# Attention's values of each head's first unit by 64 queries, in halves of the columns of TensorE's array

## The chip, the cores and the metric

One core of a Trainium2 chip runs the whole program. The metric is the device time of one execution in microseconds (us), median over several runs; the profile is of one more execution, recorded by the hardware profiler. TensorE (PE) multiplies a moving operand by weights that a separate instruction, LDWEIGHTS, has put into its 128 x 128 array; the profile shows the weight loads as an engine of their own (PEld). VectorE is DVE, ScalarE is ACT, GpSimd is POOL, and SP issues nearly all transfers.

## The reference, cut to what matters

The kernel computes a gated mix of two branches over 2048 tokens of width 576: an attention with a compressive memory (32 heads of 18 columns, four segments of 512 tokens), and a feed-forward block of 4608 hidden columns.

```python
logits = jnp.einsum("bhqd,bhkd->bhqk", qs, ks) * scale + mask   # causal, inside a segment
p = _softmax(logits, axis=-1)
a_dot = jnp.einsum("bhqk,bhkd->bhqd", p, vs)                    # the values
...
o = g * a_mem + (1.0 - g) * a_dot
...
b = (_gelu(x @ w_gate) * (x @ w_up)) @ w_down
return g * a + (1 - g) * b
```

The change is in the product of `p` with `vs`.

## The kernel before, in words

A first stage (to about 250 us) projects queries, keys and values and builds the memories. Then 144 steps (`step(v)`) run the feed-forward block, two for each block of 128 hidden columns. The attention is laid between those steps: one head of one half of the tokens for each step, 64 in all, from about 260 to 1440 us. A last stage multiplies by `wo`, mixes and stores.

A half of the tokens is two segments, so each of the 64 has two **units**, one segment each: unit `a` is `2*kk + e`, with `e` 0 for the first and 1 for the second. For a unit, `scores` (L1145) multiplies queries and keys, `powers` and `pair_rows` make the probabilities and split them in two float16 words, and `turn_rows` (L1177) has two transposing DMAs write them, turned, into the tile `pt` (128 keys x 20 blocks x 128 queries).

`values(a)` then multiplies. A unit has four blocks of 128 queries (`qi`); block `qi` needs `qi + 1` blocks of keys, and each has two words: (1 + 2 + 3 + 4) x 2 = 20 products. In each, 128 keys x 128 queries of `pt` are the weights, and the 37 columns of that head's values (`vt`: 18 low, 18 high, and a column of ones) are the moving operand. The result, 128 queries x 37, is summed in the PSUM tile `pv`. `normalize` reads it when both units are done.

In a step, `values(2k-3)` (a second unit, `e` = 1) stands early, ahead of the products of L1276. `values(2k-2)` (a first unit, `e` = 0) stands late: behind chains of the down projection (`down`, L1236, 288 columns) and ahead of `low_rests` (L1288) and `scores`, whose matmuls use only part of the array's rows (64 and 54).

The order of the instructions on PE, ACT, DVE and POOL is that of the code. SP's order is set by a scheduler, from its own estimates of when things are ready.

In the first stage, `memorize` (L745) multiplies with weights of 64 columns, in turns for the array's columns 0 to 63 and 64 to 127; the profile writes this shape as `128*64`. In each of its groups there are 15 matmuls for the lower half, of 72 or 76 columns, and 12 for the upper, of 90 or 95.

Of the kernel before, what the change touches and what calls it, by code (L numbers as in the profile page):

```python
# [18 lines left out]
P = 128  # L19
# [16 lines left out]
VC = 2 * DH + 1  # L36
# [9 lines left out]
def kernel(ctx: ExitStack, tc: tile.TileContext, xs, wqk, wv, wo, wgu, wd, beta, out):  # L46
    nc = tc.nc
    pe, act, dve, pool, sp = nc.tensor, nc.scalar, nc.vector, nc.gpsimd, nc.sync
# [6 lines left out]
    def bank(tag, bufs=1, dt=F32):  # L55
        return ps.tile([P, 512 if dt == F32 else 1024], dt, name=tag, tag=tag, bufs=bufs)
# [469 lines left out]
    with tc.tile_pool(name="prj", bufs=2, side="right", reuse_waits="tile") as pp:  # L526
# [60 lines left out]
        def project(s, j):  # L587
            w = W[j]
            i = j % 4
            if s == 0:  # L590
                i = (1, 1, 3, 4, 4, 1, 0, 3, 1)[j]
            pr = bank("dn", 2) if s and j == 0 or i == 4 else bank("G") if i == 0 else bank("U") if i == 3 else bank("st", 2)
            chain_w(pr, lambda k, a: w[:, a, k * P : (k + 1) * P], x16[s])
            return s, j, pr
# [190 lines left out]
        with tc.manual_schedule(engines=ORDERED):  # L785
# [3 lines left out]
            start = bank("G")  # L789
# [210 lines left out]
            for s in range(4):  # L1000
# [28 lines left out]
                for j in range(9):  # L1029
# [4 lines left out]
                    if s or j > 1:  # L1034
                        pr = project(s, j)
                    elif j == 0:
                        prs = project_first()
                        pr = prs[0]
                    else:
                        pr = prs[1]  # L1040
# [43 lines left out]
    with tc.tile_pool(name="keep", bufs=2, side="right", reuse_waits="tile") as kp, ExitStack() as tail:  # L1084
# [46 lines left out]
        COL = [9 * P, 7 * P, 4 * P, 0]  # L1131
# [47 lines left out]
        def values(a):  # L1179
            kk, e = divmod(a, 2)  # L1180
            if e == 0:
                pvb[kk] = bank("pv")
            o = pvb[kk]
            pr = turned_p.pop(a)
            v = vts[kk // 4]
            c0 = (kk % 4) * VC
            for qi in range(4):
                ov = o[:, (4 * e + qi) * VC : (4 * e + qi + 1) * VC]
                for kb in range(qi + 1):
                    for i in range(2):  # L1190
                        pe.matmul(ov, pr[:, 10 * i + COL[qi] // P + kb], v[:, 4 * e + kb, c0 : c0 + VC],  # L1191
                                  start=kb == 0 and i == 0, stop=kb == qi and i == 1)

        def normalize(kk):
            hf, k = divmod(kk, H)
# [168 lines left out]
        def step(v):  # L1364
# [59 lines left out]
            if on(k - 2):  # L1424
                values(2 * k - 3)
# [130 lines left out]
            if on(k - 1):  # L1556
                values(2 * k - 2)
# [279 lines left out]
```

## Time and profile before

| what | value |
|---|---|
| median of 3 runs | 1554.31 us (1554.14 to 1554.58) |
| the profiled execution's own time | 1554.45 us |
| its span, first to last instruction | 1552.7 us |
| granted TensorE clock | 1.000 |
| busy: PE, PEld | 1546.6 us, 951.4 us |
| busy: DVE, ACT, POOL | 1229.5, 1183.8, 1305.3 us |
| matmuls of the values (L1191) | 2560, of 179 ns each in the records |

A matmul's recorded duration runs from its start to the end of its way through the array. Matmuls overlap, so what one costs in a stream is the distance from its start to the next one's, which the timeline shows. The other engines' busy time matters only where PE waits for them.

### The profile page before, as it was taken

The page shows a single profiled execution, that of the slowest core. Times are in us where ns is not written, and L with a number is a line of the kernel's source. Part 1 is how long each engine was busy: PE and PEld are TensorE (multiplying, and loading weights), DVE is VectorE, ACT ScalarE, POOL GpSimd, SP SyncE. Part 2 cuts the span into 40 slices and gives each one's busy share as a digit, 9 for nine tenths or more (in the row PEclk, how much of TensorE's full clock was granted, in tenths as well). Part 3 has the DMA queues.
Part 4 walks back from the last instruction along what each step waited for, and adds up shares of the span by engine and source line. Part 5 has one row for each costly group of instructions (what it writes and reads, how often), then busy time and mean ns, then how long its engine had stood idle before and what let it go on. Part 6 is the DMA issues. An engine that isn't in the chain of part 4 may idle for free.

```text
span 1552.7 us, 34141 instructions
## 1 busy us (share of the span) xinstructions
PE 1546.6 (100%) x12303; PEld 951.4 (61%) x12304; DVE 1229.5 (79%) x3198; ACT 1183.8 (76%) x2037; POOL 1305.3 (84%) x1313
## 2 busy tenths in 40 slices
PE   9999999999999999999999999999999999999999
PEld 5665655665666666666666666666665666666577
DVE  6788976777878787878788887878787878887665
ACT  7567545888888888888888888888888888876421
POOL 3545778999898999989899989898998989899597
PEclk9999999999999999999999999999999999999999
DMA  7533341577777687778777887978687769684554
GB/s 254 198 130 125 127 150 36 121 129 137 131 138 146 127 140 129 143 129 136 131 137 126 139 140 136 135 141 151 127 138 138 139 135 134 129 141 95 123 115 138
DMA packets 472601, 210.14 MB, mean 135 GB/s; under 512 B 427632, under 2 KB 437360, under 8 KB 471920
## 3 DMA queue, kind: packets, MB, share of 16 engines
q1 hardware_dynamic: 472432, 207.97, 68.1%
q8 instruction: 96, 1.57, 0.4%
q14 instruction: 73, 0.60, 0.1%
HBM read 92.03 MB, written 27.26 MB: 77 GB/s over the span
## 4 chain that ended last, share of the span: by engine, by line
PE 92%; POOL 3%; ACT 2%; DVE 2%; issue 1%; DMA 0%; SPq 0%; POOLq 0%; DVEq 0%
PE dn L1236 27%; PE U L1276 22%; PE V L1276 12%; PE pv L1191 4%; PE G L385 3%; PE dn L454 2%; PE st L447 2%; PE U L1283 2%; PE dn L385 1%; PE V L1288 1%; PE G L1288 1%; PE st L1145 1%; PE st L1677 1%; PE G L447 1%; PE U L447 1%; PE G L1283 1%
## 5 line engine op out<-in xcount | busy, mean ns | idle before, releaser
L1236 PE MATMUL dn<-paird,hh 128*128 128x288 f16 x3396 | 476.6, 287 | 0.2
L1172 POOL TENSOR_TENSOR pf<-pf,ph 128x512 f16<-128x512 f32 (+1 forms) x256 | 359.2, 1403 | 94.5 <-ACT ph L1171 83.5
L1236 PEld LDWEIGHTS <-hh 128*128 128x128 f16 x3456 | 332.0, 98 | 139.2 <-issue 18.1
L1276 PEld LDWEIGHTS <-pairg 128*128 128x128 f16 x2616 | 243.9, 98 | 254.8 <-issue 18.3
L1244 DVE SCALAR_TENSOR_TENSOR acc<-dn,ev,acc 128x288 f32<-128x288 f32 x534 | 274.2, 514 | 51.3 <-PE dn L1236 42.8
L1161 ACT ACTIVATE pf<-pf,mb,esc 128x512 f32<-128x512 f32 (+3 forms) x512 | 293.0, 643 | 5.3
L1276 PE MATMUL U<-xt,pairg 128*128 128x512 f16 x864 | 210.0, 379 | 0.2 <-DVE gl L1467 0.2
L1276 PE MATMUL U<-x,pairg 128*128 128x512 f16 x840 | 204.2, 380 | 0.0
L426 POOL TENSOR_TENSOR pairg<-raw,pairg 128x640 f16<-128x640 f32 (+2 forms) x144 | 176.3, 1240 | 2.7 <-issue 1.5
L1171 ACT ACTIVATE ph<-pf 128x512 f16<-128x512 f32 (+1 forms) x256 | 172.4, 720 | 0.0
L1263 POOL TENSOR_TENSOR hh<-gl,hh 128x512 f16<-128x512 f32 x144 | 164.3, 1162 | 7.5 <-ACT hh L1262 7.5
L1148 DVE CUSTOM_DVE_ANT_0 pf<-st,mask 128x512 f32<-128x512 f32 (+1 forms) x256 | 157.1, 614 | 0.0
L418 ACT ACTIVATE pairg<-raw 128x640 f16<-128x640 f32 (+2 forms) x144 | 89.3, 647 | 57.0 <-POOL raw L410 36.6
L1266 ACT ACTIVATE gl<-gl,sc 128x512 f32<-128x512 f32 x144 | 97.2, 716 | 40.7 <-DVE gl L1513 30.1
L303 POOL TENSOR_SCALAR raw<-raw,sc 128x640 f32<-128x640 f32 x72 | 118.6, 1661 | 0.0
L1467 DVE COPY gl<-U 128x512 f32<-128x512 f32 x72 | 49.8, 692 | 85.5 <-PE U L1276 74.9
L1158 ACT ACTIVATE mb<-mx,esc 128x4 f32<-128x4 f32 x128 | 37.5, 293 | 103.4 <-DVE mx L1148 103.4
L1148 DVE CUSTOM_DVE_ANT_0 pf<-dn,mask 128x256 f32<-128x256 f32 (+1 forms) x192 | 67.1, 374 | 55.4 <-PE dn L1145 55.4
L1276 PE MATMUL V<-xt,pairg 128*128 128x512 f16 x432 | 105.8, 381 | 0.0
L1276 PE MATMUL V<-x,pairg 128*128 128x512 f16 x432 | 104.8, 378 | 0.0
L1262 ACT ACTIVATE hh<-gl 128x512 f16<-128x512 f32 x144 | 82.6, 616 | 16.1 <-DVE gl L1258 16.0
L1191 PEld LDWEIGHTS <-pt 128*128 128x128 f16 x2560 | 83.4, 96 | 12.3
(357 smaller groups left out, 2962.9 us busy)
## 6 DMA issues: line engine op xcount, KB each, us to landing
raw<-in_wgu_dram SPq DMA_DIRECT2D x36, 640.0 KB
rawd<-in_wd_dram SPq DMA_DIRECT2D x36, 288.0 KB
qk<-stage SPq DMA_DIRECT2D x36, 256.0 KB
qt<-qk SPq DMA_DIRECT2D x128, 72.0 KB
kt<-qk SPq DMA_DIRECT2D x128, 72.0 KB
vp<-vstage SPq DMA_DIRECT2D x16, 296.0 KB
vt<-vp SPq DMA_DIRECT2D x16, 296.0 KB
qt<-qk SPq DMA_DIRECT2D x128, 36.0 KB
```

Source lines behind the costliest of these rows:

```text
L303: pool.tensor_scalar(r, r, scl[f // 2][0][:, 0:1], None, OP.mult)
L426: pool.tensor_tensor(spot(f, *p, 1), raw_g[f][:, p[0] : p[1]], spot(f, *p, 0), OP.subtract)
L1148: dve.tensor_tensor_reduce(prob[a][:, COL[qi] : COL[qi] + (qi + 1) * P], out[qi], mask[:, L - (qi + 1) * P :], 1.0, -3e38, OP.add, OP.max, ...
L1161: act.activation(r, r, AF.Exp, bias=b[:, qi : qi + 1], scale=esc[:, 0, c : c + 1])
L1171: act.activation(h[:, cols], p[:, cols], AF.Copy)
L1172: pool.tensor_tensor(p.bitcast(F16)[:, cols], p[:, cols], h[:, cols], OP.subtract)
L1191: pe.matmul(ov, pr[:, 10 * i + COL[qi] // P + kb], v[:, 4 * e + kb, c0 : c0 + VC], start=kb == 0 and i == 0, stop=kb == qi and i == 1)
L1236: pe.matmul(o[:, :NH], hh[:, a, q * P : (q + 1) * P], w[:, b, n * NH : (n + 1) * NH], start=i == 0, stop=i == 5)
L1244: dve.scalar_tensor_tensor(av, o[:, :NH], ev, av, OP.mult, OP.add)
L1263: pool.tensor_tensor(hh[:, 1], t, hh[:, 0], OP.subtract)
L1266: act.activation(t, o, AF.Gelu_apprx_tanh, scale=scl[f // 2][0][:, 2 + c : 3 + c])
L1276: pe.matmul(o, w[:, i, (a + k) * P : (a + k + 1) * P], x[:, b + k], start=start and k == 0 and i == 0 and b == h, stop=k == 1 and i == 1, ...
```

## The change

For first units (`e` = 0), each product is made in two: queries 0 to 63 as weights in the array's columns 0 to 63, then queries 64 to 127 in columns 64 to 127. Each half has a weight load of 128 x 64 and a matmul of the same 37 columns, and writes 64 partitions of `pv`. Second units stay as they are.

```diff
                 for kb in range(qi + 1):
                     for i in range(2):
-                        pe.matmul(ov, pr[:, 10 * i + COL[qi] // P + kb], v[:, 4 * e + kb, c0 : c0 + VC],
-                                  start=kb == 0 and i == 0, stop=kb == qi and i == 1)
+                        w = pr[:, 10 * i + COL[qi] // P + kb]
+                        for r in (0, 64) if e == 0 else (None,):
+                            h = slice(0, P) if r is None else slice(r, r + 64)
+                            pe.matmul(ov[h], w[:, h], v[:, 4 * e + kb, c0 : c0 + VC],
+                                      start=kb == 0 and i == 0, stop=kb == qi and i == 1)
```

Line numbers behind this place grow by three: L1191 becomes L1194, L1236 becomes L1239, L1288 becomes L1291.

The first place is on PE, where a first unit begins, behind the down projection's last matmul. Before:

```order
L1236 LDWEIGHTS hh_2727
L1236 MATMUL dn<-paird,hh_2727 128x288
L1191 LDWEIGHTS pt
L1191 MATMUL pv<-vt,pt 128x37
L1191 LDWEIGHTS pt
L1191 MATMUL pv<-vt,pt 128x37
```

And now:

```order
L1239 LDWEIGHTS hh_2727
L1239 MATMUL dn<-paird,hh_2727 128x288
L1194 LDWEIGHTS pt
L1194 MATMUL pv<-vt,pt 64x37
L1194 LDWEIGHTS pt
L1194 MATMUL pv<-vt,pt 64x37
```

Where one product stood there are two halves. PE has 26777 rows in place of 24217: 1280 more matmuls and 1280 more weight loads. Nothing else on PE has moved, nor on DVE.

The second place is the end of the same unit, before and now:

```order
L1191 LDWEIGHTS pt
L1191 MATMUL pv<-vt,pt 128x37
L1288 LDWEIGHTS pairg_3165
L1288 MATMUL G<-x_231,pairg_3165 128x512
L1288 LDWEIGHTS pairg_3165
L1288 MATMUL U<-x_501,pairg_3165 128x512
```

```order
L1194 LDWEIGHTS pt
L1194 MATMUL pv<-vt,pt 64x37
L1291 LDWEIGHTS pairg_3165
L1291 MATMUL G<-x_231,pairg_3165 128x512
L1291 LDWEIGHTS pairg_3165
L1291 MATMUL U<-x_501,pairg_3165 128x512
```

Behind the unit follows what followed before.

The third place is SP's queue, where a step loads the next queries and keys (`qt`, `kt`) and turns a unit's probabilities (`pt`). Before:

```order
L1106 DMA qt<-qk 36x1x1024
L1177 DMA_TRANSPOSE pt<-pf_2732 128x10x128
L1177 DMA_TRANSPOSE pt<-ph 128x10x128
L1107 DMA qt<-qk 18x1024
L1108 DMA kt<-qk 36x1x1024
```

And now:

```order
L1177 DMA_TRANSPOSE pt<-ph 128x10x128
L1177 DMA_TRANSPOSE pt<-pf_2732 128x10x128
L1106 DMA qt<-qk 36x1x1024
L1107 DMA qt<-qk 18x1024
L1108 DMA kt<-qk 36x1x1024
```

In 31 of the steps one load of queries has moved behind the two transposes that it stood ahead of, and these two have changed places. No transfer is added or taken away.

## The prediction

> **What bounds the kernel.** I read the page's busy times and its chain first, then PE's waits, then the timeline around one first unit.
>
> ```profile
> PE 1546.6 (100%) x12303; PEld 951.4 (61%) x12304; DVE 1229.5 (79%) x3198; ACT 1183.8 (76%) x2037; POOL 1305.3 (84%) x1313
> ...
> PE 92%; POOL 3%; ACT 2%; DVE 2%; issue 1%; DMA 0%; SPq 0%; POOLq 0%; DVEq 0%
> ```
>
> PE is busy through the whole span and is 92% of the chain that ended last. "Busy" alone could mislead, since matmuls overlap; so here is all that PE waited for (engine, line, releaser: total us, times, longest us).
>
> ```profile
> PE G L791 <- POOL wst L787: 1.0, 1, 1.0
> PE dn L457 <- DVE wv L128: 0.4, 1, 0.4
> PE dn L683 <- DVE mo L705: 0.4, 1, 0.4
> PE dn L674 <- DMA acc<-in_wv_dram: 0.3, 1, 0.3
> PE U L1276 <- DVE gl L1467: 0.2, 1, 0.2
> ```
>
> That is 2.3 us in all, and only the last row (0.2 us) lies in the stage of the attention. The same stage as one stretch (us, PE busy and matmuls, granted clock, DMA share, GB/s):
>
> ```profile
> 300.00:1400.00 1100.00, 1100.00 (x9166) 1.00 0.77 135
> ```
>
> PE has no slack there, at full clock. Whatever a step takes longer or shorter on PE moves the end by as much, 64 times.
>
> **A first unit and a second unit now.** One step's PE timeline (start, length of the merged rows with the last one's way out, count):
>
> ```profile
> 717.92 2.40 PE L1236 MATMUL dn<-paird,hh 128*128 128x288 f16 x18
> 720.16 0.66 PE L1191 MATMUL pv<-vt,pt 128*128 128x37 f16 x20
> 720.75 0.39 PE L1288 MATMUL G<-x,pairg 64*128 64x512 f16 x1
> ...
> 723.71 1.46 PE L1276 MATMUL U<-x,pairg 128*128 128x512 f16 x6
> 725.01 0.66 PE L1191 MATMUL pv<-vt,pt 128*128 128x37 f16 x20
> 725.51 0.38 PE L1276 MATMUL V<-x,pairg 128*128 128x512 f16 x1
> ```
>
> Starts tell the cost. The second unit takes 725.51 - 725.01 = 0.50 us, 25 ns for each of 20 load-and-matmul pairs. The first unit has the same 20 but takes 720.75 - 720.16 = 0.59 us: what follows it uses half of the array's rows (`64*128`), and this change of the array's shape costs 0.09 us. On the way in there is no such loss: 18 matmuls of 288 columns take 2.24 us, 124 ns each, to the start of the unit.
>
> Two streams without a change of shape give the price of a moving column: 18 of 288 columns at 124 ns, and 6 of 512 at 1.30 / 6 = 217 ns (723.71 to 725.01), so 93 ns for 224 columns, 0.41 ns each. 37 columns are then 15 ns of streaming, and the 25 ns is a floor that something else sets. It is there for one column too:
>
> ```profile
> 11.25 0.29 PE L105 MATMUL st<-wst,onesb 128*128 128x1 bf16 x6
> 11.40 0.49 PE L674 MATMUL dn<-acc,raw 128*128 128x288 f32 x1
> ```
>
> Six in 0.15 us, 25 ns each.
>
> **What halves of the columns cost.** No row before has this shape with 37 columns, but the memory's products (L745) use it with 72 to 95.
>
> ```profile
> 63.44 0.29 PE L456 MATMUL dn<-wv,x 128*128 128x290 f16 x1
> 63.57 0.29 PE L457 MATMUL dn<-wv,x 128*128 128x290 f16 x1
> 63.78 0.55 PE L745 MATMUL U<-vstage,krow 128*64 128x76 f16 x17
> ...
> 64.17 0.34 PE L745 MATMUL pv<-vstage,krow 128*64 128x72 f16 x8
> 64.44 0.67 PE L454 MATMUL dn<-wv,x 128*128 128x288 f16 x4
> ```
>
> A matmul of 290 columns is followed after 0.13 us by its like, and after 0.21 us by the first half: going from the whole array to halves costs 0.08 to 0.09 us, as much as the change to `64*128` above. I take 0.09 for each.
>
> The rate inside the group, in a stretch that holds all 27 starts (matmuls started in brackets):
>
> ```profile
> 63.78:64.31 0.53, 0.53 (x27) 1.00 0.00 0
> ```
>
> 26 distances in 0.53 us is 20.4 ns for a half, below the floor of 25, so the halves do run beside each other. By halves: 15 in the lower, 0.53 / 14 = 38 ns from one to the next in the same half, of which some 31 ns are streaming (about 75 columns); 12 in the upper, 48 ns at about 93 columns.
>
> The weight loads, whole and half:
>
> ```profile
> L1191 PEld LDWEIGHTS <-pt x2560: 94/96/99, 285.3 to 1431.5; 128*128 128x128 f16 x197
> ```
>
> ```profile
> L745 PEld LDWEIGHTS <-krow x243: 106/109/119, 63.8 to 177.1; 128*64 128x64 f16 x122
> ```
>
> A load of half as many columns takes 109 ns where the whole one takes 96, 13 ns longer.
>
> **The sum, for one first unit.**
> 1. The way in gains a change of shape, from `128*128` to `128*64`: +0.09 us. Nothing hides it, since PE waits for nothing else there. Were it hidden (next loads pulled ahead), 0.
> 2. The unit's body: 20 steps of 25 ns now (0.50 us). After, 20 steps in which both halves run side by side. The memory's halves gain by their shape because each half needs only its own heads' columns; here both stream the same 37, so a half has as much to stream as the whole had. Lower bound: the floor holds for each half alone, 25 ns, and nothing changes. Upper bound: the 38 ns of the lower half above, which has the same loads and twice the columns, so +0.26 us. Between them I take 30 ns: streaming falls to 15 ns and no longer binds, but the load's 13 ns more will show in part. 20 x 30 = 0.60 us, +0.10.
> 3. The way out: a change of shape before (0.09), and one after; 0.
> 4. Transfers: SP's queue has one load of queries behind two transposes. The price is nothing while both are early:
>
> ```profile
> 723.88 0.61 SPq L1106 DMA_DIRECT2D qt<-qk  x1
> 727.31 1.37 SPq L1177 DMA_TRANSPOSE pt<-pf  x1
> 728.78 2.19 SPq L1177 DMA_TRANSPOSE pt<-ph  x1
> 731.02 0.49 SPq L1107 DMA_DIRECT2D qt<-qk  x1
> ```
>
> ```profile
> 737.76 0.66 PE L1191 MATMUL pv<-vt,pt 128*128 128x37 f16 x20
> ...
> 742.61 0.66 PE L1191 MATMUL pv<-vt,pt 128*128 128x37 f16 x20
> ```
>
> The transposes are out by 731, and no unit starts before 737.76. The load of queries would be issued behind them, about where its three companions for the same head were already (731.02), and these had to wait for the transposes before, too. If that cover went, PE would wait for `qt` or `pt`, and the row to show it would be PE's waits. DVE, ACT and POOL keep their instructions and get 0.19 us more for each step.
>
> So +0.19 us for each of 64 units, 12.2 us. The profiled execution took 1554.45 us (span 1552.7), 0.14 above the median of 1554.31, which is no difference here: 1566.6 us. The ends: 0.09 x 64 = 5.8, 1560.2 us; and (0.09 + 0.26) x 64 = 22.4, 1576.9 us.
>
> [...]
>
> **Rivals.**
> - *The halves shed the floor, and the way in is free* (the other side). If the 25 ns belong to the whole array, a half may go at its streaming and the few ns above it: 288 columns at 0.41 are 118 of 124 ns, so 15 + 6 = 21 to 22 ns; 20 x 22 = 0.44 us, -0.06. With the way in hidden, -3.8 us: 1550.6. For it: the 20.4 ns average at L745. Against it: the constant 0.08 to 0.09 us at the shape's change, and 25 ns at one column. It decides where 20 steps plus the way in stay under 0.50 us: with 0.09, under 20.5 ns a step.
> - *The floor is shed but the way in is paid*: 0.44 + 0.09 - 0.50 = +0.03 us, 1.9 in all: 1556.4, no change to be seen.
> - *The halves do not pair up.* The change does not do what it says: 40 pairs go one behind another at the best rate seen, 20.4 ns: 0.82 us, +0.32, with the way in +0.41, 26.2 us: 1580.6. For it: 20.4 is the fastest that the trace shows for pairs of load and matmul. Against it: at L745 that rate is explained by what each half streams (31 and 39 of 38 and 48 ns).
> - *The floor of 25 ns binds each matmul of the queue*: 40 x 25 = 1.00 us, +0.50 + 0.09, 37.8 us: 1592.2. Against it are the 20.4 ns. [...] For one whole array the trace agrees (25 ns); for halves, L745 does not.
>
> **Chances.** Body and way in as summed, between the ends: 0.82. Halves not paired at 20.4 ns: 0.07; floor for each matmul: 0.03. Floor shed, way in paid: 0.05; shed and free: 0.03. A measurement of this kernel tells 0.2%, 3.1 us, from no change. Faster 0.03, same 0.05, slower 0.92. The range is the first case's with its ends, 1560 to 1577 us; it leaves out 0.18.
>
> **What would show it.** Right: the values' first units as `128*64` with `64` result rows; about 0.21 us from the last L1239 start (288 columns) to the first half, where 0.12 was; 20 pairs in about 0.6 us, and 0.09 us behind them; half loads of about 109 ns; PE's waits as before; second units still 0.50 us. Wrong: halves at under 25 ns a step, a way in of 0.12 us, or halves that start 20 ns or more apart in turn. It would also be wrong if PE's waits name `pt` or `qt`, because of SP's new order, or if something behind PE gains.

## The result, and the profile after

The changed kernel takes 1570.10 us (median of 4 runs, 1569.79 to 1570.74) against 1554.44 us before (4 runs): 15.7 us more, a ratio of 1.0101 with a 95% interval from 1.0088 to 1.0114. It is slower by 1.0%, which is small but clear of the noise, inside the range of 1560 to 1577 us and 3.5 us above the forecast. The profiled execution took 1570.02 us (span 1568.0).

The lines of the page that answer to those shown of before, busy time and chain:

```profile
PE 1562.5 (100%) x13583; PEld 955.9 (61%) x13584; DVE 1227.2 (78%) x3198; ACT 1183.7 (75%) x2037; POOL 1306.4 (83%) x1313
...
PE 95%; POOL 2%; DVE 2%; ACT 1%; issue 1%; POOLq 0%; DVEq 0%
```

PE grew by 15.9 us of busy time and the span by 15.3; the weight loads (PEld) by 4.5; no other engine grew by more than 1.1. All waits of PE:

```profile
PE G L791 <- POOL wst L787: 1.0, 1, 1.0
PE dn L457 <- DVE wv L128: 0.4, 1, 0.4
PE dn L683 <- DVE mo L705: 0.4, 1, 0.4
PE U L1279 <- DVE gl L1470: 0.2, 1, 0.2
```

They are those of before, less one of 0.3 us. So the time lies in what PE itself does. A step's timeline on PE, as it was read before:

```profile
723.61 2.40 PE L1239 MATMUL dn<-paird,hh 128*128 128x288 f16 x18
725.94 0.81 PE L1194 MATMUL pv<-vt,pt 128*64 128x37 f16 x40
726.68 0.39 PE L1291 MATMUL G<-x,pairg 64*128 64x512 f16 x1
...
730.94 0.66 PE L1194 MATMUL pv<-vt,pt 128*128 128x37 f16 x20
731.45 0.38 PE L1279 MATMUL V<-x,pairg 128*128 128x512 f16 x1
```

From the first down-projection matmul to the first unit there were 2.24 us before and are 2.33 now: the way in, +0.09. The first unit takes 726.68 - 725.94 = 0.74 us where it took 0.59: +0.15. Second units still take 0.51. That is 0.24 us a step. The medians of the single starts over all 64 units give 0.093 + 0.152 = 0.245 us, and 64 of them are the whole 15.7 us.

The loads (line, shape, count | busy us, mean ns | idle before):

```profile
L1194 PEld LDWEIGHTS <-pt 128*64 128x64 f16 x2560 | 45.6, 113 | 15.2 <-issue 14.0 <-DMA pt<-pf 1.2
L1194 PEld LDWEIGHTS <-pt 128*128 128x128 f16 x1280 | 41.7, 96 | 9.1
```

A half load takes 113 ns, a whole one 96. The 1.2 us put down to `pt<-pf` are idle time of the loads on the way in. They cost PE nothing: the way in is the same, 0.215 to 0.216 us from start to start, in all 64 units.

### The profile page after: what moved, and what is told of

Read it like the earlier page. It is cut to its first block, busy times and chain, and to the rows that moved or that the text cites. A ratio compares the mean times of both kernels' runs of the same rounds, so it can differ in the third digit from the quotient of the medians.

```text
span 1568.0 us, 36701 instructions
## 1 busy us (share of the span) xinstructions
PE 1562.5 (100%) x13583; PEld 955.9 (61%) x13584; DVE 1227.2 (78%) x3198; ACT 1183.7 (75%) x2037; POOL 1306.4 (83%) x1313
## 4 chain that ended last, share of the span: by engine, by line
PE 95%; POOL 2%; DVE 2%; ACT 1%; issue 1%; POOLq 0%; DVEq 0%
PE dn L1239 27%; PE U L1279 23%; PE V L1279 12%; PE pv L1194 5%; PE G L385 4%; PE dn L454 2%; PE st L447 2%; PE U L1286 2%; PE dn L385 1%; PE V L1291 1%; PE G L1291 1%; PE st L1145 1%; PE st L1680 1%; PE U L447 1%; PE G L447 1%; PE V L1286 1%
## 5 line engine op out<-in xcount | busy, mean ns | idle before, releaser
L1239 PE MATMUL dn<-paird,hh 128*128 128x288 f16 x3396 | 476.5, 286 | 0.0
L1239 PEld LDWEIGHTS <-hh 128*128 128x128 f16 x3456 | 332.1, 98 | 139.1 <-issue 18.3
L1279 PEld LDWEIGHTS <-pairg 128*128 128x128 f16 x2616 | 244.0, 98 | 254.8 <-issue 18.3
L1279 PE MATMUL U<-xt,pairg 128*128 128x512 f16 x864 | 209.9, 379 | 0.2 <-DVE gl L1470 0.2
L1279 PE MATMUL U<-x,pairg 128*128 128x512 f16 x840 | 204.1, 379 | 0.0
L1279 PE MATMUL V<-xt,pairg 128*128 128x512 f16 x432 | 105.7, 381 | 0.0
L1279 PE MATMUL V<-x,pairg 128*128 128x512 f16 x432 | 104.8, 378 | 0.0
L1194 PEld LDWEIGHTS <-pt 128*64 128x64 f16 (+1 forms) x3840 | 87.3, 107 | 24.3 <-issue 14.0
L1265 ACT ACTIVATE hh<-gl 128x512 f16<-128x512 f32 x144 | 82.6, 615 | 15.7 <-DVE gl L1261 15.6
```

The source lines that it names most:

```text
L1194: pe.matmul(ov[h], w[:, h], v[:, 4 * e + kb, c0 : c0 + VC], start=kb == 0 and i == 0, stop=kb == qi and i == 1)
L1239: pe.matmul(o[:, :NH], hh[:, a, q * P : (q + 1) * P], w[:, b, n * NH : (n + 1) * NH], start=i == 0, stop=i == 5)
L1279: pe.matmul(o, w[:, i, (a + k) * P : (a + k + 1) * P], x[:, b + k], start=start and k == 0 and i == 0 and b == h, stop=k == 1 and i == 1, ...
```

## The experiments

A unit's body is compared below as (start of L1291 less the unit's first start, less 0.09 us for the change of shape behind it) / 20. Before it is (0.59 - 0.09) / 20 = 25 ns a step, and after (0.74 - 0.09) / 20 = 32.5; the trace's single starts lie 31.7 ns apart in a half, and only the first step is longer: 53 ns, where the kernel before has 28 or 29. The two halves of a step start 3 to 4 ns apart.

The times of `e1` to `e3` are medians of 4 runs; `e4` to `e8` ran once each, so their argument rests on the steps in their traces, all at a granted clock of 1.00. The kernel before took 1554.95 us (median of 7) beside `e1` to `e4`, and 1555.22 (one run) beside the others. The edits show the product alone; where queries or words are left out, `normalize` is cut to match, which is not printed.

**Is it the change of shape, or the half products?** Two kernels put halves into only one of the 20 products, the last (`e1`) or the first (`e2`). The last:

```diff
-                        for r in (0, 64) if e == 0 else (None,):
+                        for r in (0, 64) if e == 0 and qi == kb == 3 and i == 1 else (None,):
```

> Only the last of a first unit's 20 products is made in halves; the other 19 are whole. Theory (a change of the array's shape costs about 93 ns each time, and the way out costs one change before as after): the way in moves to the last product, +93 ns, the way out +7 ns as in the changed kernel, so +0.10 us for each of 64 units, +6.4 us: 1560.8 us. Rival (what costs is the half products themselves, about evenly): a twentieth of the change's 15.7 us, +0.8 us: 1555.2 us.

```profile
704.06 0.53 PE L1239 MATMUL dn<-paird,hh 128*128 128x288 f16 x3
704.43 0.78 PE L1194 MATMUL pv<-vt,pt 128*128 128x37 f16 x21
705.14 0.39 PE L1291 MATMUL G<-x,pairg 64*128 64x512 f16 x1
```

1561.71 us, +6.8, ratio 1.0043 (1.0028 to 1.0058). One product in halves costs 43% of what 20 cost. The unit takes 0.71 us, 0.12 more than before; nothing is lost ahead of it (0.12 us after the last start of L1239).

The first:

```diff
-                        for r in (0, 64) if e == 0 else (None,):
+                        for r in (0, 64) if e == 0 and qi == 0 and i == 0 else (None,):
```

> Only the first of a first unit's 20 products is made in halves; 19 whole ones follow. Theory (93 ns for each change of shape): one change into halves, one back to the whole array (from the halves' start to the next whole one some 110 to 117 ns in place of 25), and the way out as before the change: 93 + 85 to 92 ns, +0.18 us for each unit, +11.4 us: 1565.8 us. Rival (the half products cost evenly): 1555.2 us.

```profile
705.98 0.41 PE L1239 MATMUL dn<-paird,hh 128*128 128x288 f16 x2
706.32 0.79 PE L1194 MATMUL pv<-vt,pt 128*64 128x37 f16 x21
707.04 0.39 PE L1291 MATMUL G<-x,pairg 64*128 64x512 f16 x1
```

1568.19 us, +13.2, ratio 1.0084 (1.0068 to 1.0101). One product at the front costs nearly as much as all 20 in halves, since the array changes back: 138 ns from the halves' start to the next whole product, where a step takes 25. Both runs fall with the theory and far from the rival's 1555.2. Both are somewhat above its numbers (6.4 and 11.4 us): behind a single pair of halves the next shape starts 138 ns after the halves, where 110 to 117 were expected. The first halves behind a change of shape take 206 to 208 ns in the records of these kernels, in place of 185; these 21 ns more would account for the 138, but the profile models the ends of matmuls, so this is a reading and not shown.

**Both units in halves** (`e3`).

```diff
-                        for r in (0, 64) if e == 0 else (None,):
-                            h = slice(0, P) if r is None else slice(r, r + 64)
+                        for r in (0, 64):
+                            h = slice(r, r + 64)
```

> Second units in halves too. They are followed by whole-array matmuls, not by matmuls on part of the rows. Theory (every change of shape is paid): a second unit gains a way in (+93 ns), the slower body (+146 ns) and a way out (117 ns in place of 25, +92): +0.33 us for each of 64, +21.2 us over the changed kernel: 1591.3 us. Rival (halves need no way out of their own): +0.24 us each: 1585.4 us.

```profile
701.76 0.53 PE L1239 MATMUL dn<-paird,hh 128*128 128x288 f16 x3
702.22 0.81 PE L1194 MATMUL pv<-vt,pt 128*64 128x37 f16 x40
702.97 0.39 PE L1279 MATMUL V<-x,pairg 128*128 128x512 f16 x1
```

1594.97 us, +40.0, ratio 1.0257 (1.0242 to 1.0272). A second unit takes 0.75 us where it took 0.50, and the way in is paid ahead of it: its way out (117 ns in place of 25) costs as much as a way in. By the single starts that is 0.33 us for each second unit, 21.2 us, as the theory has it. But 24.3 us are added to the first units' 15.7, 3 us more than that. Most of these lie elsewhere, where L1279 follows L385 (14 times, 0.19 us longer than in the changed kernel, 2.6 us), at loads that waited for nothing that the profile shows; the first row is of this kernel, the second of the changed one (total us, times, longest):

```profile
PEld L1279 <- issue: 21.2, 83, 0.5
```

```profile
PEld L1279 <- issue: 18.3, 68, 0.5
```

What these further waits of about 0.2 us are, once in four steps, was not settled.

**What sets the step of 31.7 ns?** First with one half alone, the upper left out (`e4`):

```diff
-                        for r in (0, 64) if e == 0 else (None,):
+                        for r in (0,) if e == 0 else (None,):
```

> First units make only the half of queries 0 to 63, in columns 0 to 63; the upper half is left out (and normalize works on 64 partitions). 20 pairs of load and matmul in place of 40. Theory W (the load of 64 columns sets the step inside a half): steps stay at 31.7 ns, a unit's starts span 0.62 us, about 1570 us. Rival I (the queue hands out the four instructions of a step at about 8 ns each): half of them take half as long, down to the floor of 25 ns: 0.48 to 0.51 us, 1561 to 1563 us.

```profile
707.25 0.82 PE L1194 MATMUL pv<-vt,pt 128*64 128x37 f16 x20
708.00 0.39 PE L1291 MATMUL G<-x,pairg 64*128 64x512 f16 x1
```

1570.02 us. The unit takes 0.75 us here, and 0.74 in most of the 64, for 20 pairs as for 40: half of the instructions and nothing gained. The second half is free, and the step belongs to each half by itself.

Then with shorter loads (`e5`):

```diff
-                            h = slice(0, P) if r is None else slice(r, r + 64)
+                            h = slice(0, P) if r is None else slice(r, r + 48)
```

> Halves as in the change, but each loads only 48 of its 64 queries (16 of each half are left out; normalize works on 48 partitions). 40 pairs, 37 moving columns. Theory W (load sets the step, 0.41 ns a column and some 5 ns): 48 columns give 25 ns: a unit's starts span about 0.50 us, 0.12 less than the change, 1562.5 us. Rivals I (instructions handed out) and S (streaming and a fixed part): 31.7 ns a step as before, 1570.1 us.

```profile
703.97 0.69 PE L1194 MATMUL pv<-vt,pt 128*48 128x37 f16 x40
704.59 0.39 PE L1291 MATMUL G<-x,pairg 64*128 64x512 f16 x1
```

1561.56 us, 6.3 over before. The unit takes 0.62 us: (0.62 - 0.09) / 20 = 26.5 ns a step, with the longer first one in it. Behind the first step the single starts lie 25 ns apart in a half, as before the change. Most of what is left over before is the way in, 64 x 0.093 = 6.0 us.

And with fewer moving columns (`e6`):

```diff
-                            pe.matmul(ov[h], w[:, h], v[:, 4 * e + kb, c0 : c0 + VC],
+                            e_ = DH if e == 0 else 0
+                            pe.matmul(ov[h, e_ :], w[:, h], v[:, 4 * e + kb, c0 + e_ : c0 + VC],
```

> Halves as in the change, with 64 queries each, but only 19 of the 37 moving columns (the low words of the values are left out in first units, and normalize takes the high words alone). Theory W (load) and rival I (instructions): 31.7 ns a step, 1570.1 us. Rival S (a step is the streaming at 0.41 ns a column and a fixed 16 ns): 24 to 25 ns a step, 0.50 us, about 1562.5 us.

```profile
706.29 0.80 PE L1195 MATMUL pv<-vt,pt 128*64 128x19 f16 x40
707.02 0.39 PE L1292 MATMUL G<-x,pairg 64*128 64x512 f16 x1
```

1569.03 us. Half of the moving columns take 0.01 us off the unit, about what the last matmul's shorter streaming would be (18 columns at 0.41 ns, an estimated 7 ns). The starts inside it lie 31.7 ns apart as before. Of load, instructions and streaming, only the load is left. The whole run is 1.1 us faster than the changed kernel: by the traces 0.4 us of it lie behind the first unit's start, about what 64 units of 7 to 8 ns make, and 0.6 us ahead of it, where the edit changes nothing.

**The same slow load without a change of shape** (`e8`): the whole array, but 96 queries.

```diff
-                        for r in (0, 64) if e == 0 else (None,):
-                            h = slice(0, P) if r is None else slice(r, r + 64)
+                        for r in (0,):
+                            h = slice(0, 96 if e == 0 else P)
```

> First units with the whole array's shape, as before the change, but each load takes 96 of the 128 queries (32 left out; normalize works on 96 partitions). 20 pairs, no change of shape on the way in. Theory W, with the fast way of loading gone for anything but 128 columns: 96 columns at 0.41 ns and 5 ns are 45 ns a step, 0.90 us in place of 0.50, +25.6 us over the kernel before: 1580 us. Rival (the load is slow only in a divided array, or does not set the step): 25 ns a step, 1554.4 us.

```profile
710.20 1.05 PE L1194 MATMUL pv<-vt,pt 128*96 128x37 f16 x20
711.18 0.39 PE L1291 MATMUL G<-x,pairg 64*128 64x512 f16 x1
```

```profile
L1194 PEld LDWEIGHTS <-pt 128*96 128x96 f16 x1280 | 67.7, 125 | 1.6
L1194 PEld LDWEIGHTS <-pt 128*128 128x128 f16 x1280 | 41.7, 96 | 9.1
```

1578.44 us, 23.2 over before. (0.98 - 0.09) / 20 = 44.5 ns a step; 45 was forecast. A load of 96 columns is dearer than one of 128, and divided halves have no part in it. There is nothing lost on the way in here (0.12 us), so what costs 93 ns ahead of the halves is the change of shape and not the slower load. In every unit run here a load has as many columns as the product has rows of results, so none parts the two; but rows alone cannot be the cause, since 128 of them go at 25 ns a step and 96 at 45. Steps of 31.7 ns at 64 columns and 45.0 at 96 (single starts) give 0.416 ns for each column loaded and 5 ns.

**Quarters** (`e7`).

```diff
-                        for r in (0, 64) if e == 0 else (None,):
-                            h = slice(0, P) if r is None else slice(r, r + 64)
+                        for r in (0, 32, 64, 96) if e == 0 else (None,):
+                            h = slice(0, P) if r is None else slice(r, r + 32)
```

> First units in four quarters of 32 queries in place of two halves: 80 pairs of load and matmul for each unit, 37 columns each. Theory W (load sets the step inside a quarter): loads of 32 columns take half as long, so the step falls to the floor of 25 ns or below it and four quarters run beside each other: a unit's starts span 0.50 us or less, 1562.5 us. Rival I (about 8 ns for each instruction): 80 pairs in 1.27 us, +0.64 us for each unit, 1611 us.

```profile
707.13 0.80 PE L1194 MATMUL pv<-vt,pt 128*32 128x37 f16 x80
707.87 0.39 PE L1291 MATMUL G<-x,pairg 64*128 64x512 f16 x1
```

1569.75 us, between the two theories. Single starts tell why: the first eight steps go at 25 ns (the very first is 39), four quarters in each, as theory W has it; then the pairs come one behind another, some 8.3 ns apart, half of the 16 that rival I has for a pair. This looks like a rate of the queue's own, some 8 ns for a load and its matmul, which 40 pairs in 0.63 us do not reach and 80 do. No run was made to show it, and what sets it is open.

## Why the prediction was right, and where its sizes were off

- *PE is the bound and has no slack.* Right: the steps' 64 x 0.245 us came out as 15.7 us, and PE's waits stayed as they were.
- *The way in, +0.09 us, hidden by nothing.* Right: 2.24 to 2.33 us, and `e1` and `e2` show that it is paid for one product as for twenty. The other changes of shape at these units cost about as much: from the whole array to `64*128` there were 111 ns from start to start before, where a step takes 25 (86 more), from halves to `64*128` there are 118, where a step takes 31.7 (86 more), and from halves to the whole array 117 in `e3` (85 more) and 138 behind a single pair (113 more than a whole step). What that time is spent on the traces do not show.
- *The body, 30 ns a step, +0.10 us.* This is the term that was mis-sized: 32.5 ns and +0.15. The prediction took a value near the middle between the floor and the memory's 38 ns, on the ground that part of the 13 ns by which a half load's record is longer would show. In part is how it came: half loads are 17 ns longer in the records, and the step is 6.5 ns longer. What the prediction lacked is that the load alone sets the step (`e4` to `e6`, `e8`), at 31.7 ns with 37 moving columns and with 19; its 30 ns was a guess between two bounds. Of the +0.152 us a unit, 18 later steps make 0.118, the longer first step 0.024, which the sum did not have, and the way out 0.01. The 50 ns a unit beyond the forecast are 3 us of the 3.5 by which it was low.
- *The way out, 0.* Right within 0.01 us (117 to 118 ns for 111), and only because a change stood there already: `e3` pays it.
- *Transfers, 0.* Right: no wait of PE names `qt` or `pt`.
- *Rivals.* "Not paired" and "25 ns for each matmul of the queue" fall with the changed kernel's own starts, 3 to 4 ns apart within a step, and with `e4`, where the second half is free. "The floor is shed" is not met by `e5` alone: its 25 ns with 48 columns are also what the load would take by 5 ns + 0.416 ns a column. In `e7` the same rule would give 18 ns for 32 columns, and the quarters' first steps still take 25. So the floor belongs to each part by itself, and the lower bound of the sum was the right one to keep.
- *The price of a load.* The prediction had 109 ns for 64 columns and 96 for 128. The runs show 93, 100, 113 and 125 ns for loads of 32, 48, 64 and 96 columns (`e7`, `e5`, the changed kernel, `e8`) and 96 for one of 128, and `e8` shows that 96 columns in the whole array load slowly too, 45.0 ns a step. What the expectation of `e8` calls the fast way of loading is known here by these times alone; why a load of 128 columns goes faster than one of 96 no run shows.

## What to carry to other kernels

The gain of halves would lie in fewer moving columns for each half than the whole had; the memory's products are made so, but no run here compares them with whole ones. Where both halves stream the same columns, as here, nothing is saved, and what is short already (37 columns under a floor of 25 ns) meets a slower load (113 ns in place of 96, and 31.7 ns a step). Count the changes of the array's shape around a group first (85 to 93 ns each at these units, 113 behind a single pair), and put a group of a new shape only where a change stands anyway. When a term lies between two bounds, ask which resource would set it, and price that one, rather than take the middle.

## What was not expected of the hardware

The step of a load and its matmul was the larger of 25 ns and 5 ns + 0.416 ns for each column loaded, at 32, 48, 64 and 96 columns (25 in the first eight steps, 25, 31.7 and 45.0 ns), while steps with whole loads of 128 columns kept to 25.3: a step with a load of three quarters of the array takes nearly twice one with all of it. The rule's two numbers are fitted to 64 and 96 columns; 48 and 32 do not contradict it, and nothing between 96 and 128 was run. The floor is no limit on the array as a whole: two halves ran at one matmul in 16 ns, four quarters at one in 6 to 7 ns for the first 32, and at one in about 8 behind them.
